# Plain loads of the next batch between the two crossbar parts of a batch, with three smaller moves in the first batch

## The chip, the cores and the metric

The kernel runs on one core of one Trainium2 chip. The metric is the device time of one execution in microseconds; 366.56 us is the median of three runs of the kernel before (366.42 to 367.95).

## The reference

Two stages follow each other. The first is attention with 8 batches, 8 heads, 576 positions and a head size of 64. Heads 0 to 3 ("plain") see the last 32 positions; heads 4 to 7 ("dilated") see every fourth of the last 128. The second is a gated feed-forward block (FFN) over 8 x 576 = 4608 tokens.

```python
B, H, S, D = q.shape                       # 8, 8, 576, 64
scores = (1 / sqrt(D)) * q @ k.transpose(0, 1, 3, 2)
rel = pos[:, None] - pos[None, :]
mask_plain = (rel >= 0) & (rel < 32)                       # heads 0..3
mask_dil = (rel >= 0) & (rel < 128) & (rel % 4 == 0)       # heads 4..7
attn = softmax(where(mask, scores, -1e9)) @ v
x = attn.transpose(0, 2, 1, 3).reshape(B * S, H * D)       # 4608 x 512
g, val = x @ w_gate, x @ w_val                             # 512 -> 1536
out = (gelu(g) * val) @ w_out                              # 1536 -> 512, float32
```

All inputs and the output are float32.

## The kernel before, in words

**Attention** is cut into 32 pairs of heads, n = 0 to 31; batch b is n // 4, so that n = 4b and 4b + 1 are the plain pairs of batch b, and 4b + 2 and 4b + 3 the dilated ones. `emit_s` computes the scores of a pair on TensorE (PE) from transposed q and k and takes their exp on ScalarE (ACT); `emit_pv` computes the numerator (probabilities times v) and the denominator (probabilities times ones); `norm_r` and `norm_x` divide on VectorE (DVE) and write `xT`, the input of the FFN with its 512 channels on the partitions of four tiles, one per pair of a batch. `den` and `num` do the two halves separately for batches 0 and 1.

**The FFN** runs over 9 chunks c of 512 tokens. `ffn1` computes gate and value for one of 12 blocks nb of 128 hidden units into two banks of PSUM (the accumulators, 8 banks), `geglu` forms the product `u_all` on ACT and DVE, and `ffn2` multiplies it with `w_out` for the four groups of 128 tokens; `store` copies a result to one of four `osb` buffers and writes it out from SyncE's queue (SP). `ffn1_two` is the form that takes the first two blocks together, channel tile by channel tile, so that it can begin before all of `xT` is there; it is used for the first blocks of chunks 0 to 2. The scores of later pairs are put between the matmuls of earlier chunks by lists (`in_a`, `in_b`): n = 4 to 7 within chunk 0, 8 to 12 at and after the end of chunk 1's first half, 13 to 19 in chunk 2, 20 to 23 in chunk 3, and so on. PE takes all of it in the order in which it is written.

**Loading a batch b >= 2** has several parts. Float32 rows of q, k for the plain heads come to the tile `st` in 10 transfers, those of v to `sv` in 5, all from SP (`load_batch_plain`: L185 and L173). The dilated rows come to `qd` and `rd` by casting transfers from GpSimd's queue (POOL), and `st` is cast to `qp` by POOL (L190, L191). Then SP issues the crossbar transposes, DMA transfers that transpose fp16 data: two for the dilated heads (`qd`, `rd` to `qTd`: L218, L219) and five for the plain heads (`qp` to `qTp`: L223). At last POOL loads the dilated v (`vd`, `vr`) and casts `sv` (L177, L178). The tiles `st`, `sv`, `qp`, `qd` and `rd` have one buffer each, the transposed tiles two, and those of v three. `last_keys` copies the last 64 keys of the dilated heads to `kTr`; it is done on VectorE (L245) except for batch 0, where it is on POOL, behind the issue of the weights' transfers.

The order of all queues is written by hand (`manual_schedule`); the framework adds the waits. A DMA queue takes its transfers in the order written:

```python
if c in (1, 2, 3):
    load_batch(c + 2)          # plain loads, dilated loads, cast, crossbar, v
if c == 4:
    load_batch(7)
...
    if c == 3 and nb == 5:
        load_batch(6)
```

Batch 2 is loaded in two halves, its plain loads ahead of chunk 0 (`half2`) and the rest after chunk 0's first half. Batch 0 and the q, k of batch 1 are transposed on PE. The first pairs of batch 0 are in this order: den 1, scores 2, den 2, scores 3, num 0 in banks 4 and 5, num 1 in banks 0 and 1, den 3, num 2 in banks 2 and 3, num 3 in banks 4 and 5; `ffn1_two` of chunk 0 uses banks 0, 1, 6 and 7.

Of the kernel before, what the change touches and what calls it, by code (L numbers as in the profile page):

```python
# [38 lines left out]
def kernel(  # L39
# [10 lines left out]
    nc = tc.nc  # L50
# [109 lines left out]
    def new_v(b):  # L160
        vp = vpl.tile([P, 4, HK, D], F16, tag="vp", name=f"vp{b}")
        vd = vpl.tile([P, HK, 4, D], F16, tag="vd", name=f"vd{b}")

        vt = vpl.tile([P, HK, D], F16, tag="vt", name=f"vt{b}")
        vr = vpl.tile([P, HK, 2, D], F16, tag="vr", name=f"vr{b}")
        sv = ldp.tile([P, 5, HK, D], F32, tag="sv", name=f"sv{b}")
        tiles["v", b] = (vp, vd, vt, vr)
        return sv

    def v_plain(b, sv, eng):  # L170
        for kb in range(5):
            k0 = min(kb * P, S - P)
            gated(eng.dma_start(out=sv[:, kb], in_=v[b, 0:HK, k0 : k0 + P, :].rearrange("h p d -> p h d")))  # L173
# [6 lines left out]
    def load_qk_plain(b):  # L180
        st = ldp.tile([P, 5, 2, HK, D], F32, tag="st", name=f"st{b}")
        for t, src in ((0, q), (1, k)):
            for kb in range(5):
                n, sr = rows(src, b, kb)
                gated(nc.sync.dma_start(out=st[0:n, kb, t], in_=sr))  # L185
        return st

    def cast_qk_plain(b, st):
        qp = ldp.tile([P, 5, 2, HK, D], F16, tag="qp", name=f"qp{b}")
        nc.gpsimd.tensor_copy(qp[:, 0:4], st[:, 0:4])  # L190
        nc.gpsimd.tensor_copy(qp[0:64, 4], st[0:64, 4])  # L191
        return qp

    def load_qk_dil(b):
        qd = ldp.tile([P, 2, HK, 4, D], F16, tag="qd", name=f"qd{b}")
        rd = ldp.tile([16, 2, HK, 4, D], F16, tag="rd", name=f"rd{b}")
        for t, src in ((0, q), (1, k)):
            nc.gpsimd.dma_start(out=fl(qd[:, t]), in_=quads(src, b, HK, 0, 4 * P))
        for t, src in ((0, q), (1, k)):
            nc.gpsimd.dma_start(out=fl(rd[:, t]), in_=quads(src, b, HK, 4 * P, S))  # L200
        return qd, rd

    def load_v_dil(b):
        nc.gpsimd.dma_start(out=fl(tiles["v", b][1]), in_=quads(v, b, HK, 0, 4 * P))
        load_v_dil_rest(b)
# [5 lines left out]
                in_=quads(v, b, HK, S - 256, S)[:, :, 2 * m * D : 2 * m * D + 2 * D],  # L211
            )

    def crossbar(b, qp, qd, rd):
        new_qt(b)
        qtp_, qtd_, ktr = tiles["qT", b]
        dst = qtd_.rearrange("p t h m i -> p (t h m) i")
        nc.sync.dma_start_transpose(out=dst[:, :, 0:P], in_=qd.rearrange("p t h r d -> p (t h r d)"))  # L218
        nc.sync.dma_start_transpose(out=dst[:, :, P:NCL], in_=rd.rearrange("p t h r d -> p (t h r d)"))  # L219
        dst = qtp_.rearrange("p t h c -> p (t h) c")  # L220
        for kb in range(5):
            n = min(P, S - kb * P)
            nc.sync.dma_start_transpose(  # L223
                out=dst[:, :, kb * P : kb * P + n], in_=qp[0:n, kb].rearrange("p t h d -> p (t h d)")
            )

    def load_batch_plain(b):
        st = load_qk_plain(b)
        sv = new_v(b)
        v_plain(b, sv, nc.sync)  # L230
        return st, sv

    def load_batch_rest(b, st, sv):
        qd, rd = load_qk_dil(b)
        qp = cast_qk_plain(b, st)
        crossbar(b, qp, qd, rd)
        load_v_dil(b)
        v_cast(b, sv)

    def load_batch(b):  # L240
        load_batch_rest(b, *load_batch_plain(b))

    def last_keys(b, h0, h1, eng=nc.vector):
        _, qtd_, ktr = tiles["qT", b]
        eng.tensor_copy(ktr[:, h0:h1], qtd_[:, 1, h0:h1, :, NCL - 64 : NCL])  # L245


    def is_plain(n):
# [332 lines left out]
    def num(n, b0):  # L581
        emit_pv(n, b0, ("num",))
        norm_x(n, b0)
# [7 lines left out]
        t_dil(0, hp, qd0, 4096 + 1024 * hp, 4608 + 1024 * hp, ("act", "dve"))  # L591
    for hp in range(2):
        t_rest(0, hp, first_r, P * hp)
    last_keys(0, 0, HK, nc.gpsimd)
    den(1, 4, wide=True)
    emit_s(2, 0, pe_mask=True)
    den(2, 4, wide=True)
    emit_s(3, 0, pe_mask=True)
    num(0, 4)
    num(1, 0)  # L600
    den(3, 4, wide=True)
    num(2, 2)
    num(3, 4)


    gate["dma"] = w1
# [15 lines left out]
    load_v_dil(1)  # L622
    v_cast(1, sv1)
    gate["dma"] = wo2
    half2 = load_batch_plain(2)

    mm0 = 0
    in_a = {2: ((4, 12),), **{c: tuple(zip((1, 3, 5, 7), range(NHP * (c + 1), NHP * (c + 2)))) for c in range(3, B - 1)}}
    in_b = {0: range(4, 8), 1: range(8, 13), 2: range(13, 20), **{c: range(NHP * (c + 2), NHP * (c + 3)) for c in range(3, B - 2)}}
    for c in range(NCH):  # L630
        if c in (1, 2, 3):
            load_batch(c + 2)
        if c == 4:
            load_batch(7)
        pv_at = dict(in_a.get(c, ()))
        s_list = list(in_b.get(c, ()))
        pairs = (mm0, mm0 + 2)
        SB = 4 - mm0

        masks = []  # L640
        pend = None
        for nb in range(NNB):
            if nb == 0 and c < 2:
                ffn1_two(c, (0, 6) if c == 0 else (6, 0))
            elif nb == 0 and c == 2:
                ffn1_two(c, pairs)
            elif nb > 1 or c > 2:
                ffn1(c, nb, pairs[(nb + (c < 2 or c == 3)) % 2])
            if pend is not None:
                norm_x(pend, SB)  # L650
                pend = None
            if nb in pv_at:
                pend = pv_at[nb]
                emit_pv(pend, SB, wide=True)
                norm_r(pend, SB, wide=True)
            if c == 0 and nb in (8, 9):
                t_plain(1, q61, nb - 8, 4 + 2 * (nb - 8), ("act", "dve"))
            if c == 0 and nb in (10, 11):
                rr = rd1.rearrange("p t h r d -> p t (h r d)")
                hp = nb - 10  # L660
                t_dil(1, hp, qd1, 4096 + 512 * hp, 5120 + 512 * hp, ("dve", "dve"))
                t_rest(1, hp, (rr[:, 0], rr[:, 1]), 6144 + P * hp)
            if c == 3 and nb == 5:
                load_batch(6)
            if nb == NNB - 1 and c > 0 and s_list:
                masks.append(emit_s(s_list.pop(0), SB))

        def s_next():
            if s_list:
                n = s_list.pop(0)  # L670
                masks.append(emit_s(n, SB, pe_mask=n in (6, 7)))

        def mask_next():
            mask = masks.pop(0) if masks else None
            if mask is not None:
                mask()

        def norm(n, b0):
            norm_r(n, b0)
            norm_x(n, b0)  # L680


        V = mm0 + 1

        def md(n):
            mask_next()
            den(n, 0, wide=True)

        if c == 0:
            load_batch_rest(2, *half2)  # L690
            ffn2(c, 0, 0, {5: [s_next]})
            store(c, 0, 0, "act")
            ffn2(c, 1, 1, {4: [s_next], 8: [lambda: md(4)]})
            store(c, 1, 1, "act")
            s_next()
            ffn2(c, 2, 0, {4: [lambda: md(5)], 6: [s_next], 9: [lambda: md(6)]})
            store(c, 2, 0, "act")
            ffn2(c, 3, 1, {2: [lambda: md(7), lambda: num(4, 4)], 8: [lambda: num(5, 6)]})
            store(c, 3, 1, "act")
            num(6, 2)  # L700
            num(7, 4)
        elif c in (1, 2):

            v0 = 8 if c == 1 else 13

            def pv(n, more=True):
                emit_pv(n, V)
                if more:
                    mask_next()
                norm(n, V)  # L710

            mask_next()
            ffn2(c, 0, V)
            store(c, 0, V, "act")
            s_next()
            ffn2(c, 1, mm0, {6: [lambda: pv(v0)]})
            store(c, 1, mm0, "act")
            s_next()
            ffn2(c, 2, mm0, {4: [lambda: pv(v0 + 1)]})
            store(c, 2, mm0, "act")  # L720
            s_next()
            ffn2(c, 3, mm0, {2: [lambda: pv(v0 + 2)], **({8: [s_next]} if c == 2 else {})})
            store(c, 3, mm0, "act")
            s_next()
            if c == 1:
                pv(v0 + 3, False)
                mm0 = 4 - mm0
            else:
                s_next()
            while masks:  # L730
                mask_next()
        else:
            mask_next()
            ffn2(c, 0, mm0)
            store(c, 0, mm0, "act")
            ffn2(c, 1, mm0 + 1, {5: [s_next]})
            mask_next()
            store(c, 1, mm0 + 1, "act")
            ffn2(c, 2, mm0 + 2, {0: [s_next]})
            mask_next()  # L740
            ffn2(c, 3, mm0 + 3, {0: [s_next]})
            mask_next()
            store(c, 2, mm0 + 2, "act")
            store(c, 3, mm0 + 3, "dve")
# [28 lines left out]
```

## Time and profile before

| what | value |
|---|---|
| median of three runs | 366.56 us |
| profiled execution, own time | 368.56 us |
| its span, first to last instruction | 366.4 us |
| PE busy | 343.0 us (94%) |
| VectorE, ACT, POOL busy | 195.4, 143.5, 76.7 us |
| SP's queue of transfers (q1) | 31.21 MB, 41.2% of 16 engines' span |
| POOL's queue of transfers (q0) | 12.01 MB, 26.9% |
| chunk 0 begins (first `ffn1_two` matmul) | 31.54 us |
| chunk 1 begins | 72.59 us |
| chunk 2 begins | 113.76 us |
| first store's issue | 80.62 us |

The profiled execution is one of its own, with its own time; 2.2 us of it lie outside the span. Times in the profile count from the span's start. "SPq" rows are transfers as SP issues them: their length is the issue, and the landing comes later and is given apart. In brackets after a row stands how long its engine was idle before it, and what ended that. A digit of a busy row is the busy share, in tenths, of one of 40 slices of 9.16 us.

### The profile page before, as it was taken

How to read it: one execution, taken by the hardware profiler on the slowest of the kernel's cores; microseconds unless marked ns; L12 is line 12 of the kernel's file. 1: busy time of each engine (PE TensorE's matmuls, PEld its weight loads, DVE VectorE, ACT ScalarE, POOL GpSimd, SP SyncE). 2: the span in 40 equal slices, each digit the busy share in tenths (PEclk: the TensorE clock that was granted, in tenths of full speed). 3: DMA queues.
4: the chain of work that ended last, by engine and by line, in shares of the span. 5: the costliest groups of instructions: out<-in, count | busy, mean ns of one | idle time of the engine just before them, and what ended most of it. 6: DMA issues, size and time to landing. Idle time of an engine off the chain costs nothing.

```text
span 366.4 us, 5947 instructions
## 1 busy us (share of the span) xinstructions
PE 343.0 (94%) x2340; PEld 162.6 (44%) x2340; DVE 195.4 (53%) x294; ACT 143.5 (39%) x209; POOL 76.7 (21%) x105
## 2 busy tenths in 40 slices
PE   6739999999997999899799999999999999999995
PEld 2515454444443444444344444444444444444442
DVE  1537455843486636789446963696269504303320
ACT  2613346343535254642463256325632313322321
POOL 2680424530630620035062060000000000000000
PEclk9856999999999999999999999999999999999999
DMA  8999999999999991289999996100110020011002
GB/s 211 226 195 225 172 164 179 185 173 247 168 160 226 181 160 59 86 184 160 162 179 150 258 171 134 59 0 3 58 58 0 2 105 10 2 58 57 2 29 86
DMA packets 107291, 45.30 MB, mean 124 GB/s; under 512 B 83040, under 2 KB 102496, under 8 KB 107264
## 3 DMA queue, kind: packets, MB, share of 16 engines
q1 hardware_dynamic: 84272, 31.21, 41.2%
q0 software_dynamic: 21456, 12.01, 26.9%
q10 hardware_dynamic: 1536, 1.70, 2.0%
q8 instruction: 18, 0.29, 0.4%
q14 instruction: 9, 0.07, 0.1%
HBM read 40.13 MB, written 9.44 MB: 135 GB/s over the span
## 4 chain that ended last, share of the span: by engine, by line
PE 67%; DMA 12%; SPq 8%; DVE 5%; POOL 3%; issue 2%; ACT 2%; ACTq 0%; POOLq 0%; DVEq 0%
PE ps L485 35%; PE ps L516 22%; DMA qTp<-qp 4%; SPq L223 4%; PE ps L437 4%; DMA xT<-in_k_dram 3%; SPq L185 3%; PE ps L497 2%; DMA sv<-in_v_dram 2%; DMA out_dram<-osb 2%; PE ps L364 1%; DVE xT L473 1%; DVE u_all L510 1%; PE ps L334 1%; DMA st<-in_k_dram 1%
## 5 line engine op out<-in xcount | busy, mean ns | idle before, releaser
L509 ACT ACTIVATE g<-ps 128x512 f16<-128x512 f32 x108 | 64.0, 597 | 131.9 <-PE ps L485 125.6
L510 DVE SCALAR_TENSOR_TENSOR u_all<-g,ps 128x512 f16<-128x512 f16 x108 | 73.9, 688 | 75.6 <-PE ps L485 68.6
L485 PE MATMUL ps<-xT,wg 128*128 128x512 f16 x408 | 104.9, 379 | 0.2
L485 PE MATMUL ps<-xT,wv 128*128 128x512 f16 x408 | 104.7, 379 | 0.0
L516 PE MATMUL ps<-wo,u_all 128*128 128x512 f16 x432 | 100.1, 380 | 1.7 <-ACT osb L527 1.2
L485 PEld LDWEIGHTS <-wv 128*128 128x128 f16 x408 | 39.9, 98 | 48.1
L516 PEld LDWEIGHTS <-u_all 128*128 128x128 f16 x432 | 39.6, 98 | 46.5 <-issue 1.8
L485 PEld LDWEIGHTS <-wg 128*128 128x128 f16 x408 | 38.2, 98 | 46.1 <-issue 2.5
L527 ACT ACTIVATE osb<-ps 128x512 f32<-128x512 f32 x30 | 17.9, 597 | 43.1 <-PE ps L516 43.1
L455 DVE STREAM_TRANSPOSE dt<-ps 128x576 f32<-128x576 f32 x32 | 24.9, 779 | 12.1 <-PE ps L437 11.5
L190 POOL CAST qp<-st 128x2048 f16<-128x2048 f32 x6 | 11.4, 1903 | 87.7 <-DMA st<-in_k_dram 87.7
L366 ACT ACTIVATE P<-ps 128x1152 f16<-128x1152 f32 x16 | 18.0, 1128 | 19.3 <-PE ps L364 19.3
L459 DVE STREAM_TRANSPOSE rb<-rc 128x576 f32<-128x576 f32 x32 | 24.9, 778 | 1.1
L374 DVE TENSOR_TENSOR P<-P,mask_p 128x1344 f16<-128x1344 f16 x14 | 12.7, 906 | 22.2 <-ACT P L345 22.2
L529 DVE TENSOR_SCALAR osb<-ps 128x512 f32<-128x512 f32 x6 | 4.2, 692 | 30.9 <-PE ps L516 30.9
L344 ACT ACTIVATE P<-ps 128x960 f16<-128x960 f32 x16 | 15.5, 970 | 9.5 <-PE ps L334 9.4
L473 DVE TENSOR_TENSOR xT<-ps,rb 128x576 f16<-128x576 f32 x16 | 17.9, 1125 | 0.2
L374 DVE TENSOR_TENSOR P<-P,mask_d 128x1152 f16<-128x1152 f16 x12 | 10.5, 874 | 12.1 <-ACT P L366 12.1
L437 PE MATMUL ps<-P,ones 128*64 128x288 f16 (+5 forms) x188 | 15.1, 267 | 1.6 <-ACT P L366 1.2
L470 DVE TENSOR_TENSOR xT<-ps,rb 128x576 f16<-128x576 f32 x16 | 11.9, 750 | 1.2 <-PE ps L437 1.1
L334 PE MATMUL ps<-qTp 64*128 64x160 f16 (+2 forms) x160 | 8.0, 221 | 4.1 <-DMA qTp<-qp 4.1
L177 POOL CAST vp<-sv 128x1024 f16<-128x1024 f32 x8 | 8.9, 1107 | 10.9 <-DMA sv<-in_v_dram 10.9
(74 smaller groups left out, 238.0 us busy)
## 6 DMA issues: line engine op xcount, KB each, us to landing
out_dram<-osb SPq DMA_DIRECT2D x36, 256.0 KB, 2.0
sv<-in_v_dram SPq DMA_DIRECT2D x40, 128.0 KB, 3.5
st<-in_q_dram SPq DMA_DIRECT2D x24, 128.0 KB, 5.3
st<-in_k_dram SPq DMA_DIRECT2D x24, 128.0 KB, 3.3
qd<-in_q_dram POOLq DMA_DIRECT2D x7, 256.0 KB, 5.7
qd<-in_k_dram POOLq DMA_DIRECT2D x7, 256.0 KB, 7.3
vd<-in_v_dram POOLq DMA_DIRECT2D x7, 256.0 KB, 6.5
wg<-in_moe_w_gate_dram POOLq DMA_DIRECT2D x3, 512.0 KB, 7.7
```

The source lines that it names most:

```text
L344: nc.scalar.activation(pt[:, :, 0:PB], sb[:, 0, :, 0:PB], AF.Exp, bias=0.0, scale=scale)
L366: nc.scalar.activation(pt, ps[:, b0 : b0 + 4, 0:DW], AF.Exp, bias=0.0, scale=scale)
L374: nc.vector.tensor_tensor(pt, pt, mb, ALU.mult)
L437: nc.tensor.matmul(o, lhs, rhs, start=st, stop=True, skip_group_check=True)
L455: nc.vector.transpose(dst, den)
L459: nc.vector.transpose(rb.rearrange("p (b c) -> p b c", c=32), bass.AP(tensor=rc.tensor, offset=rc.offset, ap=[rc.ap[0], [1, 18], [0, 32]]),)
L473: nc.vector.tensor_tensor(dst.rearrange("p (i m s) -> p i m s", m=2, s=2), num, rb.rearrange("p (s m i) -> p i m s", s=2, m=2), ALU.mult,)
L485: nc.tensor.matmul(ps[:, b0 + gi, :], w[:, kc, ns], xT[kc][:, tok], start=(kc == 0), stop=(kc == NKC - 1))
L509: nc.scalar.activation(g, ps[:, b0, :], AF.Gelu)
L510: nc.vector.scalar_tensor_tensor(u_all[:, nb, :], g, USCALE, ps[:, b0 + 1, :], ALU.mult, ALU.mult)
L516: nc.tensor.matmul(ps[:, bank, :], u_all[:, fc, tb * P : (tb + 1) * P], wo_t[fc // 4][:, fc % 4, :], start=(fc == 0), stop=(fc == NNB - 1),)
L527: nc.scalar.activation(osb, ps[:, bank, :], AF.Copy, bias=0.0, scale=1.0 / USCALE)
```

## The change

`load_batch_rest` becomes the one function for batches 2 to 7. It issues the two dilated transposes of batch b, then the 15 plain loads of batch b + 1 (if there is one), then the five plain transposes of batch b. So batch b + 1 no longer has plain loads at its own place in the chunk loop. POOL's part of a batch keeps its order; its program text stands ahead of the transposes. Three moves concern the first batch: its last keys are copied by VectorE; num 0 comes ahead of den 2, num 1 ahead of den 3 and in banks 4 and 5, num 2 and num 3 in banks 0, 1 and 2, 3; and `ffn1_two` of chunk 0 takes banks 4 to 7. The number of transfers and of matmuls is the same.

```diff
--- before.py
+++ after.py
@@ -211,12 +211,26 @@
                 in_=quads(v, b, HK, S - 256, S)[:, :, 2 * m * D : 2 * m * D + 2 * D],
             )
 
-    def crossbar(b, qp, qd, rd):
+    def load_batch_plain(b):
+        st = load_qk_plain(b)
+        sv = new_v(b)
+        v_plain(b, sv, nc.sync)
+        return st, sv
+
+    def load_batch_rest(b):
+
+        st, sv = tiles["plain", b]
+        qd, rd = load_qk_dil(b)
+        qp = cast_qk_plain(b, st)
+        load_v_dil(b)
+        v_cast(b, sv)
         new_qt(b)
-        qtp_, qtd_, ktr = tiles["qT", b]
+        qtp_, qtd_, _ = tiles["qT", b]
         dst = qtd_.rearrange("p t h m i -> p (t h m) i")
         nc.sync.dma_start_transpose(out=dst[:, :, 0:P], in_=qd.rearrange("p t h r d -> p (t h r d)"))
         nc.sync.dma_start_transpose(out=dst[:, :, P:NCL], in_=rd.rearrange("p t h r d -> p (t h r d)"))
+        if b + 1 < B:
+            tiles["plain", b + 1] = load_batch_plain(b + 1)
         dst = qtp_.rearrange("p t h c -> p (t h) c")
         for kb in range(5):
             n = min(P, S - kb * P)
@@ -224,25 +238,9 @@
                 out=dst[:, :, kb * P : kb * P + n], in_=qp[0:n, kb].rearrange("p t h d -> p (t h d)")
             )
 
-    def load_batch_plain(b):
-        st = load_qk_plain(b)
-        sv = new_v(b)
-        v_plain(b, sv, nc.sync)
-        return st, sv
-
-    def load_batch_rest(b, st, sv):
-        qd, rd = load_qk_dil(b)
-        qp = cast_qk_plain(b, st)
-        crossbar(b, qp, qd, rd)
-        load_v_dil(b)
-        v_cast(b, sv)
-
-    def load_batch(b):
-        load_batch_rest(b, *load_batch_plain(b))
-
-    def last_keys(b, h0, h1, eng=nc.vector):
+    def last_keys(b, h0, h1):
         _, qtd_, ktr = tiles["qT", b]
-        eng.tensor_copy(ktr[:, h0:h1], qtd_[:, 1, h0:h1, :, NCL - 64 : NCL])
+        nc.vector.tensor_copy(ktr[:, h0:h1], qtd_[:, 1, h0:h1, :, NCL - 64 : NCL])
 
 
     def is_plain(n):
@@ -591,16 +589,16 @@
         t_dil(0, hp, qd0, 4096 + 1024 * hp, 4608 + 1024 * hp, ("act", "dve"))
     for hp in range(2):
         t_rest(0, hp, first_r, P * hp)
-    last_keys(0, 0, HK, nc.gpsimd)
+    last_keys(0, 0, HK)
     den(1, 4, wide=True)
     emit_s(2, 0, pe_mask=True)
+    num(0, 4)
     den(2, 4, wide=True)
     emit_s(3, 0, pe_mask=True)
-    num(0, 4)
-    num(1, 0)
+    num(1, 4)
     den(3, 4, wide=True)
-    num(2, 2)
-    num(3, 4)
+    num(2, 0)
+    num(3, 2)
 
 
     gate["dma"] = w1
@@ -622,16 +620,16 @@
     load_v_dil(1)
     v_cast(1, sv1)
     gate["dma"] = wo2
-    half2 = load_batch_plain(2)
+    tiles["plain", 2] = load_batch_plain(2)
 
     mm0 = 0
     in_a = {2: ((4, 12),), **{c: tuple(zip((1, 3, 5, 7), range(NHP * (c + 1), NHP * (c + 2)))) for c in range(3, B - 1)}}
     in_b = {0: range(4, 8), 1: range(8, 13), 2: range(13, 20), **{c: range(NHP * (c + 2), NHP * (c + 3)) for c in range(3, B - 2)}}
     for c in range(NCH):
         if c in (1, 2, 3):
-            load_batch(c + 2)
+            load_batch_rest(c + 2)
         if c == 4:
-            load_batch(7)
+            load_batch_rest(7)
         pv_at = dict(in_a.get(c, ()))
         s_list = list(in_b.get(c, ()))
         pairs = (mm0, mm0 + 2)
@@ -641,7 +639,7 @@
         pend = None
         for nb in range(NNB):
             if nb == 0 and c < 2:
-                ffn1_two(c, (0, 6) if c == 0 else (6, 0))
+                ffn1_two(c, (4, 6) if c == 0 else (6, 0))
             elif nb == 0 and c == 2:
                 ffn1_two(c, pairs)
             elif nb > 1 or c > 2:
@@ -661,7 +659,7 @@
                 t_dil(1, hp, qd1, 4096 + 512 * hp, 5120 + 512 * hp, ("dve", "dve"))
                 t_rest(1, hp, (rr[:, 0], rr[:, 1]), 6144 + P * hp)
             if c == 3 and nb == 5:
-                load_batch(6)
+                load_batch_rest(6)
             if nb == NNB - 1 and c > 0 and s_list:
                 masks.append(emit_s(s_list.pop(0), SB))
 
@@ -687,7 +685,7 @@
             den(n, 0, wide=True)
 
         if c == 0:
-            load_batch_rest(2, *half2)
+            load_batch_rest(2)
             ffn2(c, 0, 0, {5: [s_next]})
             store(c, 0, 0, "act")
             ffn2(c, 1, 1, {4: [s_next], 8: [lambda: md(4)]})
```

## The prediction

> **What bounds the kernel now.** I read the page first, then PE's waits, PE's timeline, SP's timeline and the chain of waits.
>
> ```profile
> PE 343.0 (94%) x2340; PEld 162.6 (44%) x2340; DVE 195.4 (53%) x294; ACT 143.5 (39%) x209; POOL 76.7 (21%) x105
> DMA  8999999999999991289999996100110020011002
> ```
>
> PE is the engine with little idle time (366.4 - 343.0 = 23.4 us). The DMA row is full from slice 1 to 14 (9 to 137 us) and again from 165 to 220: in those stretches a transfer put ahead of another makes the other late.
>
> ```profile
> PE ps L364 <- POOL kTr L245: 4.3, 1, 4.3
> PE ps L334 <- DMA qTp<-qp: 4.1, 3, 1.9
> ...
> 24.06 0.21 PE L364 MATMUL ps<-qTd,kTr 64*128 64x32 f16 x2 [4.34 <-POOL kTr L245]
> ...
> 93.71 0.47 PE L334 MATMUL ps<-qTp 64*128 64x160 f16 x10
> ...
> 112.50 0.20 PE L334 MATMUL ps<-qTp 64*128 64x64 f16 x2 [1.48 <-DMA qTp<-qp]
> ...
> 180.86 0.20 PE L334 MATMUL ps<-qTp 64*128 64x64 f16 x2 [1.93 <-DMA qTp<-qp]
> ```
>
> These are PE's two largest waits and four places of its timeline. The scores of head pair n take batch n // 4. 93.71 is n=8 (batch 2; no wait), 112.50 is n=12 (batch 3; 0.73 + 1.48 us of waiting), 180.86 is n=20 (batch 5). So at the end of chunk 1 PE has **no slack** against the plain crossbar transposes of batch 3, at the end of chunk 3 none against those of batch 5.
>
> ```profile
> 69.19 3.52 SPq L218 DMA_TRANSPOSE qTd<-qd  x1
> 72.83 1.15 SPq L219 DMA_TRANSPOSE qTd<-rd  x1
> 74.08 6.45 SPq L223 DMA_TRANSPOSE qTp<-qp  x5
> 80.62 2.75 SPq L531 DMA_DIRECT2D out_dram<-osb  x4
> 83.42 5.30 SPq L185 DMA_DIRECT2D st<-in_q_dram  x5
> 88.77 3.61 SPq L185 DMA_DIRECT2D st<-in_k_dram  x5
> 92.48 2.76 SPq L173 DMA_DIRECT2D sv<-in_v_dram  x5
> 95.84 2.83 SPq L218 DMA_TRANSPOSE qTd<-qd  x1
> 98.79 1.15 SPq L219 DMA_TRANSPOSE qTd<-rd  x1
> 100.04 6.43 SPq L223 DMA_TRANSPOSE qTp<-qp  x5
> ```
>
> SP's queue from batch 2 to batch 3 has no pause: each row starts where the last ends. Not PE but this queue sets 112.45. The chain of waits says the same:
>
> ```profile
> 80.62 6.31 DMA out_dram<-osb
> 86.94 1.78 SPq L185
> ...
> 105.27 7.18 DMA qTp<-qp
> ```
>
> A store issued at 80.62 lands at 86.93, just after the last transpose before it (79.33 + 7.0 = 86.3, landing from the tile view of qTp). The fifth load of st, eight transfers after that store, issues at that moment: as built, nearly every transfer of SP waits for the landing of the one eight before it.
>
> **The Trainium skill.** "DMA: Bandwidth & Descriptors", Queues, rings and completion order, says that each DMA engine consumes descriptors in ring order and that SP has one row of rings; the store above agrees. Its section Issuing engines are not separate DMA queues says that transfers of all issuers share 16 engines; the trace agrees (the last qTp of batch 2 takes 7.0 us with POOL's qd loads issued at 78.0, the first, ahead of them, 4.4). "TensorE: Matmul & The Clock Gate", Part 1, says that an idle window of about 3.4 us halves the clock and some 3.4 us of work restores it; PE's timeline shows 0.50 from about 16 to 33 us, with matmuls of 512 columns spaced 0.43 us in place of 0.216.
>
> **The change, part by part.**
>
> *Start.* POOL's copy of kTr (661 ns at 23.34, behind four weight issues) becomes one on VectorE: 286 ns, the mean of the seven others there. VectorE is idle for 0.41 us after the qTd copies (17.94 to 18.36), so the copy fits and den(1) is not delayed. Scores n=2 then run at about 19.7, not 24.06: minus 4.34. num(0) and num(1) fill PE's waits for exp (1.23, 0.52); the new banks 4 to 7 of the first FFN step are free in time (norm_x(1) near 25.4, the den(3) read near 26.6). I set FFN start at 27.4 against 31.54: minus 4.1 to 4.9, taken as 4.3. Weights allow it (wv: 16.39 + 8.8 = 25.2). Batch 1's casts end at 43.2 and 44.7 for transposes that would come at 43.7 and 45.9; wo2 lands at 53.1 for a use near 54. So chunk 1 also runs 4.3 early. It lasts only until PE next waits for SP.
>
> *n=8.* SP's new order from 72.83 is: qTd rest of batch 2, 15 plain loads of batch 3, five qTp of batch 2, four stores, two qTd of batch 3, 15 loads of batch 4, five qTp of batch 3. One st tile remains, so the first load waits for the cast of batch 2, done at 70.6: no wait. sv needs the casts that end at 73.9: none. The price of 15 loads: 14 x 128 KB = 1.835 MB at 196 GB/s (mean of 72.6 to 113.76) is **9.4 us**. Checks: 15 loads took 12.4, 11.4, 9.9 and 12.6 us of SP's time at 83.42, 110.79, 153.13 and 173.77; the floor is 15 x 0.51 = 7.7. qTp of batch 2 moves from 86.3 to 95.7. PE comes to n=8 at 93.7 - 4.3 = 89.4 and waits 6.3: the start's gain is gone. Behind it in PE's queue are all of chunk 1's second FFN matmuls, and ACT and VectorE wait for those.
>
> *n=12.* Before, qTp of batch 3 had stores and loads 3 ahead of it; now it has the same **and loads 4**, 15 more transfers: 112.45 + 9.4 = 121.9. The earlier st of batch 3 does not help, since its cast writes the one qp tile, which is free only when qTp of batch 2 has landed (95.7). Cast then 98.2, while stores and qTd of batch 3 still fill the ring, so no further bubble. PE comes to n=12 at 95.7 + 16.1 = 111.8 and waits 10.1 in place of 2.2. After such a wait the clock is at half: about 3.4 us of slow matmuls, **plus 1.7** (estimate by the clock page; from 0, if it holds, to 3.4).
>
> *After n=12.* A batch of SP and DMA work takes 26.7 us before (74.08 to 100.04 to 126.79), so qTp of batch 4 lands near 149; n=16 needs it near 150.5 + 11 = 161. No wait. In chunk 3 the loads of batch 5 have gone into the idle stretch of 137 to 153; loads of batch 6 take their place ahead of qTp of batch 5, but POOL's v loads (0.75 MB) leave this stretch. It lands near 187 for a use near 190: the wait of 1.93 goes, **minus 1.9** (0 to 1.9). The last batch has no loads between its crossbars; four stores after six earlier transfers still precede any reuse of osb. Nothing later waits for DMA. At the end nothing changes.
>
> *Sum.* 9.4 + 1.7 - 1.9 = **+9.2 us**, on the profiled span 366.4. That execution took 368.56 in all (2.2 outside the span), 2.0 above the median 366.56; I add the difference to the median: **375.8**.
>
> **Rivals.**
>
> *Issue-bound, not slower.* If only SP's issue counts and rings keep up: 73.98 + 7.7 + 6.5 + 1.6 + 4.1 + 7.7 + 6.4 = 108.0, and the last qTp, issued at 106.8, lands 3.4 later (the shortest landing of batch 2): 110.2. With the queue's 50 ns pauses that is about 111.5 and the total minus 1.0 minus 1.9: **363.7**. The loads taken before to 95.24 needed 11.8 us where 7.7 would do, and might lose their waits for stores. It decides if 15 loads cost under about 8 us of ring time together with POOL's qd loads. Against it: DMA is full until 137, and qd loads now meet the plain loads.
>
> *Contention twice.* Each block of loads costs 12.6 (as at 173.77, behind transposes, under POOL's loads), and the first block's excess is not caught up: qTp of batch 3 near 126, plus 1.7, and n=20 keeps its wait: **381.9**. For it: the row at 173.77. Against it: part of that time is waiting for transposes that the chain pays anyway.
>
> *The start's edit does nothing.* If n=2 found another wait (exp, weights), PE would come to n=8 later, but still before 95.7 for any loss up to 6.3: total **375.8** all the same. That gain shows only where DMA has slack, which it has not.
>
> **How the numbers follow.** Forecast 0.73 (370 to 381), issue-bound 0.13 (362 to 367), contention twice 0.12, all else 0.02. An unknown of some 4 us either side of +9.2 (loads 7.4 to 12.6, clock 0 to 3.4, n=20 0 to -1.9) gives the forecast's own range. 368 to 382 leaves out the issue-bound case and little above. About 0.5% is what a measurement of this kernel can tell from no change. Faster 0.10, same 0.05 (partly hidden loads), slower 0.85.
>
> **What would show it.** In the changed profile: no wait of PE for kTr and FFN start near 27.4; a PE wait for qTp of 4 to 8 us near 90 and one of 8 to 13 near 112, then a PEclk digit below 9; SP's loads between the two kinds of transpose taking 8 to 13 us; no wait at n=20. Wrong if qTp of batch 3 lands by 113, or if the chain no longer passes through qTp before the second chunk's end.

## The result, and the profile after

The changed kernel is **slower**: 378.93 us (median of four runs, 375.96 to 379.29) against 366.62; the ratio of the means is 1.031, with a 95% interval of 1.0252 to 1.0368. The forecast was 375.8, with a range of 368 to 382. The profiled execution took 378.67 us, 376.9 of it span. A ratio counts only executions within 1.5% of the fastest of the same kernel, which leaves out six of e1's 12 and eleven of e5's 22 below; a median counts them all.

The page of the changed kernel, rows for PE, its clock and DMA:

```profile
PE 348.3 (92%) x2340; PEld 163.8 (43%) x2340; DVE 196.6 (52%) x295; ACT 143.5 (38%) x209; POOL 76.6 (20%) x104
PEclk9959999999697799999999999999999999999999
DMA  8999999999996994549989994100110020011002
```

The same matmuls now take 5.3 us more busy time (348.3 against 343.0): in slices 10 to 13 (94 to 132 us) the clock row has a 6 and two 7s that were not there. In the DMA row slices 15 to 17 have a 4, a 5 and a 4 where they had a 1, a 2 and an 8, and slice 12 (113 to 122 us) has a 6 where it had a 9.

PE's waits and its timeline in the changed kernel (in brackets the idle time before a row):

```profile
PE ps L332 <- DMA qTp<-qp: 13.4, 8, 5.6
...
91.24 0.24 PE L332 MATMUL ps<-qTp 64*128 64x160 f16 x2 [2.49 <-DMA qTp<-qp]
...
94.84 0.24 PE L332 MATMUL ps<-qTp 64*128 64x64 f16 x2 [0.73 <-DMA qTp<-qp]
95.01 5.30 PE L514 MATMUL ps<-wo,u_all 128*128 128x512 f16 x12
...
118.28 0.32 PE L332 MATMUL ps<-qTp 64*128 64x160 f16 x2 [5.59 <-DMA qTp<-qp]
...
121.93 0.24 PE L332 MATMUL ps<-qTp 64*128 64x64 f16 x2 [0.74 <-DMA qTp<-qp]
```

The wait for `kTr` is gone, and waits for `qTp` have grown from 4.1 to 13.4 us. They stand at n=8 (5.2 us in four pieces) and at n=12 (8.2 us in four pieces), as the transposes land one after the other. The 12 matmuls behind n=8 take 5.30 us, where the same row took 2.75 before: the clock is at half. There is no wait at n=20 any more.

The stretch around n=12 in steps of 2 us. After the length of a step stand PE's busy time with its matmuls, the clock that PE was granted, the time of the DMA packets begun in the step as a share of 16 engines' time (packets overlap, so it can pass 1), and GB/s:

```profile
110.00:112.00 2.00, 2.00 (x24) 1.00 1.33 245
112.00:114.00 2.00, 0.68 (x4) 1.00 0.67 141
114.00:116.00 2.00, 0.00 (x0) 1.00 0.97 216
116.00:118.00 2.00, 0.00 (x0) 0.83 0.70 127
118.00:120.00 2.00, 0.63 (x4) 0.50 0.59 117
120.00:122.00 2.00, 0.49 (x6) 0.50 0.30 62
122.00:124.00 2.00, 2.00 (x24) 0.50 1.03 381
```

The clock falls in the fifth microsecond after PE ran out of work at 112.7. And DMA is not full while PE waits: its share lies between 0.30 and 0.97, after 1.33 just before.

SP's queue in the changed kernel:

```profile
73.80 4.00 SPq L185 DMA_DIRECT2D st<-in_q_dram  x5
77.84 3.65 SPq L185 DMA_DIRECT2D st<-in_k_dram  x5
81.59 4.54 SPq L173 DMA_DIRECT2D sv<-in_v_dram  x5
86.18 7.52 SPq L237 DMA_TRANSPOSE qTp<-qp  x5
...
100.92 4.30 SPq L185 DMA_DIRECT2D st<-in_q_dram  x5
105.26 5.08 SPq L185 DMA_DIRECT2D st<-in_k_dram  x5
110.44 3.85 SPq L173 DMA_DIRECT2D sv<-in_v_dram  x5
114.34 6.45 SPq L237 DMA_TRANSPOSE qTp<-qp  x5
```

Two blocks of 15 loads stand ahead of the plain transposes of batch 3 where one stood before. They hold SP for 12.4 us (73.80 to 86.18) and 13.4 us (100.92 to 114.34). The chain of waits passes from these transposes to PE:

```profile
107.56 2.79 SPq L185
...
119.54 2.34 DMA qTp<-qp
121.93 0.24 PE ps L332 x2
```

The last `qTp` of batch 3 is issued at 119.54 and lands at 119.54 + 2.34 = 121.88. One load, at 107.56, holds the queue for 2.79 us.

### The profile page after: what moved, and what is told of

Read it like the earlier page. It is cut to its first block, busy times and chain, and to the rows that moved or that the text cites. A ratio compares the mean times of both kernels' runs of the same rounds, so it can differ in the third digit from the quotient of the medians.

```text
span 376.9 us, 5936 instructions
## 1 busy us (share of the span) xinstructions
PE 348.3 (92%) x2340; PEld 163.8 (43%) x2340; DVE 196.6 (52%) x295; ACT 143.5 (38%) x209; POOL 76.6 (20%) x104
## 4 chain that ended last, share of the span: by engine, by line
PE 59%; DMA 14%; SPq 13%; DVE 7%; POOL 4%; issue 2%; ACT 1%; ACTq 0%; POOLq 0%; DVEq 0%
PE ps L483 34%; PE ps L514 18%; SPq L185 6%; SPq L173 4%; DMA xT<-in_k_dram 3%; PE ps L435 3%; SPq L237 3%; DMA sv<-in_v_dram 3%; DMA st<-in_k_dram 3%; DMA wv<-in_moe_w_val_dram 3%; PE ps L495 2%; DMA wo<-in_moe_w_out_dram 1%; DVE u_all L508 1%; DVE xT L471 1%; DMA qTp<-qp 1%
## 5 line engine op out<-in xcount | busy, mean ns | idle before, releaser
L514 PE MATMUL ps<-wo,u_all 128*128 128x512 f16 x432 | 102.7, 387 | 1.2 <-ACT osb L525 1.2
L453 DVE STREAM_TRANSPOSE dt<-ps 128x576 f32<-128x576 f32 x32 | 24.9, 779 | 13.4 <-PE ps L435 12.8
L372 DVE TENSOR_TENSOR P<-P,mask_p 128x1344 f16<-128x1344 f16 x14 | 13.7, 979 | 28.1 <-ACT P L343 28.1
L332 PE MATMUL ps<-qTp 64*128 64x160 f16 (+2 forms) x160 | 9.0, 227 | 13.4 <-DMA qTp<-qp 13.4
L332 PEld LDWEIGHTS <-qTp 64*128 64x128 f16 x160 | 5.5, 95 | 21.6 <-DMA qTp<-qp 10.7
```

What stands on the lines that cost most here:

```text
L372: nc.vector.tensor_tensor(pt, pt, mb, ALU.mult)
L453: nc.vector.transpose(dst, den)
L514: nc.tensor.matmul(ps[:, bank, :], u_all[:, fc, tb * P : (tb + 1) * P], wo_t[fc // 4][:, fc % 4, :], start=(fc == 0), stop=(fc == NNB - 1),)
```

## The experiments

The theory under test, **order**: what stands ahead of the plain transposes of batch 3 in SP's queue sets the start of chunk 2, and with it the end. Its rivals: the time comes from DMA being full wherever the loads stand; the moves of the first batch carry part of it; PE's clock, or a collision of engines, does.

One table first. Chunk 2 begins with the first matmul of its `ffn1_two`; "rest" is the span minus that moment. All are from one profiled execution each.

| kernel | chunk 2 begins | span | rest |
|---|---|---|---|
| before | 113.76 | 366.4 | 252.6 |
| changed | 123.25 | 376.9 | 253.7 |
| e1, e9: loads after the transposes | 111.58, 109.83 | 364.1, 362.1 | 252.5, 252.3 |
| e2: start moves only | 112.64 | 365.5 | 252.9 |
| e3: loads moved only | 124.31 | 378.1 | 253.8 |
| e4: only v between | 113.93 | 365.3 | 251.4 |
| e5, e10: and chunk 0's stores late | 108.68, 111.70 | 360.9, 365.4 | 252.2, 253.7 |
| e6: changed, with added matmuls | 122.92 | 374.8 | 251.9 |
| e7: changed, with a cast held | 121.76 | 374.9 | 253.1 |
| e8: start moves, with added matmuls | 113.34 | 365.4 | 252.1 |
| e11: e5, and v after the transposes | 109.10 | 361.2 | 252.1 |

The rest lies within 2.4 us in all of them, the start of chunk 2 within 15.6 us. Most of what decides is done by the start of chunk 2. Two executions of one kernel differ there by 1.75 us (e1, e9) and 3.02 (e5, e10), so smaller differences between single profiles show nothing.

**e1, the loads after the plain transposes.** In `load_batch_rest`:

```diff
-        if b + 1 < B:
-            tiles["plain", b + 1] = load_batch_plain(b + 1)
         dst = qtp_.rearrange("p t h c -> p (t h) c")
         for kb in range(5):
...
+        if b + 1 < B:
+            tiles["plain", b + 1] = load_batch_plain(b + 1)
```

> The changed kernel with one edit: the 15 plain loads of batch b+1 stand after the five plain transposes of batch b, not ahead of them. Order theory (the loads ahead of the plain transposes are what makes qTp late): qTp of batch 2 lands near 86 and of batch 3 near 112, PE waits 0 at n=8 and some 8 us at n=12 (it arrives 5.7 us early and the transfers do not), no wait at n=20; total about 364 to 365. Start rival (the moves of the first batch are worth their 5.7 us whenever the loads don't interfere): 360 to 361. Contention rival (any earlier load of a batch hurts, wherever it stands, since DMA is full): 372 or more.

Measured: a median of 368.73 us (363.05 to 372.32) against 366.86 for the kernel before in the same series, and a ratio of 0.9983 (0.9945 to 1.002). The median lies 0.5% above the kernel before and the ratio 0.2% below it: no difference from it can be told. The loss of 3% is gone. PE's timeline of e1:

```profile
107.47 0.30 PE L332 MATMUL ps<-qTp 64*128 64x160 f16 x4 [0.30 <-DMA qTp<-qp]
110.33 0.20 PE L332 MATMUL ps<-qTp 64*128 64x64 f16 x2 [2.56 <-DMA qTp<-qp]
```

Moving the 15 loads over five transposes gives back 11.7 us at the start of chunk 2 in the profile: no wait at n=8, none at n=20, the last `qTp` of batch 3 landed at 110.3. That refutes the contention rival in its strong form, since the loads are still earlier than before. POOL's part of a batch stands where the changed kernel has it, so its new place in the program is not the cause either. PE waited 2.9 us at n=12 and not 8, for two reasons: the transposes landed 2.2 us earlier than in the kernel before (112.45), and PE arrived near 107 and not 104. I had carried the whole 5.7 us of the start to n=12, but of 4.6 us at chunk 0 (26.91 against 31.54) 3.7 were left at n=8 (90.05 against 93.71) and 2.8 at n=12 (106.86 against 109.68). The total of 364 to 365 was missed by the profiled execution (366.07) and by the median: long executions exist, and their cause in this kernel is open.

**e9, the same kernel, a second profile.**

> The kernel with the loads after the plain transposes once more, for a second profile, since its times lie between 363 and 372 us. Order theory: in a long execution the wait at n=12 (or n=8) is longer by what the time is longer, with a half clock after it. Rival (VectorE and POOL collide): the wait at n=12 is the same and mask products of about 2 us hold PE elsewhere.

It fell on a short execution (364.05 us; waits for `qTp` of 0.6 us), so it doesn't tell what the long ones of e1 do.

**e2, only the moves of the first batch**, on the kernel before:

```diff
-    last_keys(0, 0, HK, nc.gpsimd)
+    last_keys(0, 0, HK)
...
-    num(0, 4)
-    num(1, 0)
+    num(1, 4)
...
-                ffn1_two(c, (0, 6) if c == 0 else (6, 0))
+                ffn1_two(c, (4, 6) if c == 0 else (6, 0))
```

> The kernel before with only the moves of the first batch (last keys on VectorE, order and banks of the numerators and of the first FFN step). Order theory: chunk 0 begins at 25.8 in place of 31.5, but PE meets the same qTp of batch 3 at 112.5: wait of about 8 us at n=12, total 366 to 367, no gain that can be measured. Rival (the gain of the start reaches the end): 361.

Measured: 368.37 us, a ratio of 1.0046 (1.0019 to 1.0073). Chunk 0 begins at 26.84 in place of 31.54, chunk 2 at 112.64 in place of 113.76, and its first scores (n=13) at 135.63 in place of 135.75. The gain of the start does not reach the end; the kernel is even slower by 0.5%. In PE's timeline of e2, n=12 waits 4.3 us in place of 2.2, not the 8 that were expected:

```profile
108.02 0.25 PE L334 MATMUL ps<-qTp 64*128 64x160 f16 x2 [1.50 <-DMA qTp<-qp]
110.60 0.30 PE L334 MATMUL ps<-qTp 64*128 64x160 f16 x4 [2.34 <-DMA qTp<-qp]
111.38 0.20 PE L334 MATMUL ps<-qTp 64*128 64x64 f16 x2 [0.48 <-DMA qTp<-qp]
```

**e3, only the new place of the loads**: the diff of the change without the three moves of the first batch.

> The kernel before with only the new place of the plain loads; the first batch as before. Order theory: qTp of batch 3 lands near 122 as in the changed kernel, PE arrives later and waits less, total 376 to 379, the same as the changed kernel. Rival (start moves carry part of the time): differs from the changed kernel by 4 to 6 us, to 382 to 384.

Measured: 379.18 us, a ratio of 1.0333 (1.0295 to 1.0371), the same as the changed kernel's 1.031. The last `qTp` of batch 3 lands at 122.9. The loads' place carries the whole loss, the start moves none of it that these runs can tell.

**e4, a dose: only v's five loads between.**

```diff
         if b + 1 < B:
-            tiles["plain", b + 1] = load_batch_plain(b + 1)
+            sv1_ = new_v(b + 1)
+            v_plain(b + 1, sv1_, nc.sync)
         dst = qtp_.rearrange("p t h c -> p (t h) c")
...
+        if b + 1 < B:
+            tiles["plain", b + 1] = load_qk_plain(b + 1), sv1_
```

> The changed kernel, but of the 15 plain loads only the 5 of v stand between the two kinds of transposes; the 10 of q and k come after the plain transposes. Order theory with the bytes as price: 640 KB at 196 GB/s = 3.3 us later than with none, qTp of batch 3 near 115 to 116, total near 368 to 369, a third of the way from the order with none between to the changed kernel. Rival (a threshold: what counts is the wait of the loads for st, cast or the eight transfers in flight, not the amount): no shift at all (364 to 365) or the whole one (376 and more).

Measured: 368.70 us, a ratio of 1.0055 (1.0035 to 1.0076). Chunk 2 begins at 113.93, 2.4 us after e1's 111.58 and 4.1 after e9's; the changed kernel is 11.7 and 13.4 after them. In these profiles 5 of 15 transfers (640 of 1792 KB) cost 20 to 31% of the shift, neither none nor all of it: that speaks for the amount and against a threshold. The times do not confirm it. The medians of e4 and e1 can't be told apart, so the rival's "no shift" is refuted by the profiles alone, and the last `qTp` landed at 112.6, short of the expected 115 to 116.

**e5, chunk 0's four stores behind the plain transposes of batch 3**, on e1, with seven `osb` buffers in place of four:

```diff
-        nc.sync.dma_start(out=out[t0 : t0 + P, :], in_=osb)
+        if c == 0:
+            late.setdefault(3, []).append(lambda: nc.sync.dma_start(out=out[t0 : t0 + P, :], in_=osb))
+        else:
+            nc.sync.dma_start(out=out[t0 : t0 + P, :], in_=osb)
```

> Loads after the plain transposes, as in the first experiment, and chunk 0's four stores (1 MB) moved behind the plain transposes of batch 3, with seven osb buffers in place of four. Order theory (every transfer ahead of qTp of batch 3 costs its ring time): 1 MB less ahead is 3 to 5 us less, qTp of batch 3 lands near 106 to 108, PE waits 1 to 3 us at n=12, total 360 to 363. Rival (PE-bound once the loads are out of the way): the same 364 to 367 as without the moved stores.

Measured: a median of 365.96 us (360.61 to 367.95) against 366.94, and a ratio of 0.9925 (0.99 to 0.9951). By the median that is 0.3% below the kernel before, by the ratio 0.75%; the median lies where the rival put it. In the profile, a short execution, the last `qTp` of batch 3 lands at 106.5, as the theory had it, and PE waits for none at n=12. The added buffers alone were not tried.

**e10, the same kernel, a second profile.**

> The kernel with chunk 0's stores late once more, for a second profile, since its times lie between 360 and 368 us. Order theory: a long execution has a wait for qTp of batch 3 at n=12 that the first profile of it (360.9 us of span) did not have. Rival: no such wait, and the time lies in chunk 0 or in mask products.

This one is long, 367.35 us. PE's timeline of e10:

```profile
108.17 0.30 PE L335 MATMUL ps<-qTp 64*128 64x160 f16 x4 [2.34 <-DMA qTp<-qp]
109.73 0.20 PE L335 MATMUL ps<-qTp 64*128 64x64 f16 x2 [1.26 <-DMA qTp<-qp]
111.70 0.59 PE L498 MATMUL ps<-xT,wg 128*128 128x512 f16 x1 [1.11 <-ACT P L345]
```

The wait at n=12 is back, and the first matmul of chunk 2 takes 0.59 us, at half clock. The last `qTp` landed 3.2 us later than in e5's profile, chunk 2 begins 3.0 us later, its first scores 5.6 (136.26 against 130.67), and 4.5 of it are left in the span. The same code thus waits for these transfers in one execution and not in another: in this pair, that is the spread. Why the transfers came later is open.

**e11, also v behind the transposes**, on e5, for batches 3 to 7:

```diff
-        load_v_dil(b)
-        v_cast(b, sv)
...
+        if b > 2:
+            sv = new_v(b)
+            v_plain(b, sv, nc.sync)
+            load_v_dil(b)
+            v_cast(b, sv)
```

> The kernel with chunk 0's stores late, and the v loads (plain, dilated) and casts of batches 3 to 7 behind their own batch's plain transposes: another 640 KB from SP and 512 + 256 KB from POOL less ahead of qTp of batch 3. Order theory: qTp of batch 3 lands 3 to 6 us earlier, no wait at n=12 in any execution, 360 to 362. Rival (PE is the bound by then, or v now comes late for the first numerators of batch 3): 363 or more.

Measured: 363.17 us (360.75 to 365.49), a ratio of 0.9887 (0.9836 to 0.9939). It is the fastest version found, 1.1% below the kernel before; against e5 the intervals overlap. The total lies on the rival's side of 363. In the profile the last `qTp` of batch 3 lands at 101.8, 4.7 us before e5's, as the theory had it, and PE does not wait for it; but chunk 2 begins no earlier (109.10 against 108.68). What PE waits for there is VectorE (0.87 us) and ACT (0.94): the queue has stopped being the limit.

**e6, the clock.** 40 matmuls of ones ahead of the scores of n=12, in the changed kernel:

```diff
+            if c == 1:
+                warm(40, 4)
             s_next()
```

> The changed kernel with 40 matmuls of ones (8.6 us of PE work into a bank that n=12 overwrites) put ahead of the scores of n=12, where PE waits anyway. Clock theory (the wait drops PE's clock and 2 us of chunk 2 are lost to it): no digit below 9 in the clock row near 122 to 128, the first FFN step of chunk 2 takes 3.5 us and not 5.3, total 2 us below the changed kernel, 376 to 377. Rival (the loss after the wait comes from elsewhere, or the added work delays n=12): no change or more, 378 to 381.

Measured: 376.88 us, a ratio of 1.0284 (1.0233 to 1.0335). The intervals of e6 and of the changed kernel overlap, so the total settles nothing. The profile does. PE's timeline of e6:

```profile
111.49 8.80 PE L533 MATMUL ps<-ones 128*128 128x512 f16 x40
120.22 0.57 PE L332 MATMUL ps<-qTp 64*128 64x160 f16 x8
121.67 0.20 PE L332 MATMUL ps<-qTp 64*128 64x64 f16 x2 [0.87 <-DMA qTp<-qp]
122.92 0.38 PE L495 MATMUL ps<-xT,wg 128*128 128x512 f16 x1 [0.40 <-ACT P L342]
```

The last transpose lands when it did (121.6), and chunk 2 begins within 0.3 us of when it did, but its first matmul takes 0.38 and not 0.61 us. The first FFN step lasts 3.85 us (122.92 to 126.77) against 5.78 in the changed kernel (123.25 to 129.03): the half clock cost 1.9 us there. The rest of the span is shorter by 1.8.

**e8, the same on e2**, with 22 matmuls.

> The kernel with only the moves of the first batch, and 22 matmuls of ones (4.7 us) ahead of the scores of n=12. Clock theory (the start's gain is turned into a longer wait at n=12, which drops the clock and makes that kernel 1 to 2 us slower than before): total 366 to 367, 1.5 us below the same kernel without them. Rival (qTp of batch 3 itself comes later in that kernel): no change, near 368.

Measured: 367.25 us, a ratio of 1.0001 (0.998 to 1.0022) against e2's 1.0046 (1.0019 to 1.0073). By the medians, work that computes nothing makes e2 faster by 1.1 us; the two intervals just touch. The profiles show where: in e2 chunk 2 begins 1.12 us before that of the kernel before and its first scores only 0.12 us, so the half clock took 1.0; in e8 the two leads are 0.42 and 0.43. That explains why nothing is left of the start's gain. That e2 is 0.5% slower is not explained by it, and stays open: e2's profiled span is no longer than that of the kernel before (365.5 and 366.4), nor than e8's (365.4).

**e7, a collision.** The cast of batch 5 waits for chunk 2's last store:

```diff
-        nc.gpsimd.tensor_copy(qp[:, 0:4], st[:, 0:4])
+        cast = nc.gpsimd.tensor_copy(qp[:, 0:4], st[:, 0:4])
+        if b == 5:
+            tc.add_manual_dep(cast.ins, tiles["st_c2"].ins.name, SYNC, reason="order of casts")
```

> The changed kernel with one added dependency: POOL's cast of batch 5's q and k waits for the last store of chunk 2 (near 165 us), and so does all of POOL behind it. Collision theory (VectorE's two mask products of 2.23 us near 150 and the PE wait of 0.97 us at 157 come from POOL's casts at 149 to 156): those products take 0.76 to 0.86 again, the PE wait is gone, total 1 us below the changed kernel. Rival (they come from elsewhere): products stay long, total the same; or the later cast holds up the loads of batch 6 and qTp of batch 5, and the total rises by 1 us or more.

The timelines of VectorE and POOL in the changed kernel:

```profile
149.73 2.23 DVE L372 TENSOR_TENSOR P<-P,mask_p 128x1344 f16<-128x1344 f16 x1 [1.67 <-ACT P L343]
152.05 2.23 DVE L372 TENSOR_TENSOR P<-P,mask_d 128x1152 f16<-128x1152 f16 x1
...
149.35 1.89 POOL L190 CAST qp<-st 128x2048 f16<-128x2048 f32 x1 [15.03 <-DMA qTp<-qp]
151.19 1.24 POOL L191 CAST qp<-st 64x512 f16<-64x512 f32 x1
```

and VectorE in e7:

```profile
148.07 0.86 DVE L374 TENSOR_TENSOR P<-P,mask_p 128x1344 f16<-128x1344 f16 x1 [1.67 <-ACT P L345]
150.39 0.76 DVE L374 TENSOR_TENSOR P<-P,mask_d 128x1152 f16<-128x1152 f16 x1 [1.46 <-ACT P L366]
```

Measured: 377.05 us, a ratio of 1.0302 (1.0254 to 1.0351): no difference in the total that these runs can tell. Inside, the two products are short again and PE's wait of 0.97 us at 157 is gone. From n=13 to n=17 PE takes 14.64 us (145.54 to 160.18), as in the kernel before (14.63), and not 15.68: the collision is real and cost 1.05 us. In exchange 0.49 us of waiting at n=20 are back, and a later product, at 165, takes 2.08 us beside the moved cast. The rest falls by 0.5 us (253.65 to 253.14), which is too little for single profiles to show.

## Why the prediction was right, point by point

*What bounds the kernel.* Right: no slack at n=12, and SP's queue sets that moment, as e1 and e3 show. One reading was too wide. The forecast said that nearly every transfer of SP waits for the landing of the one eight before it. That held for two loads (86.35 and 86.94) of the kernel before. In the changed kernel the load at 107.56 held SP for 2.79 us though the transfer eight before it had landed at 106.78. What makes single loads take over 2 us to issue is open.

*Start.* Forecast 27.4 for the first FFN matmul, measured 25.83; the copy of `kTr` on VectorE took no place on the path. That the gain would be lost is shown by e2 and e3. In e2 a part of it (1.0 us) goes to the clock, which the forecast did not have. The third rival said 375.8 for a start that gains nothing, and e3, which has no such gain, has the changed kernel's time.

*n=8.* Forecast: `qTp` of batch 2 at 95.7, PE there at 89.4. Measured 94.8 (92.45 + 2.35) and 88.75; the waits come to 5.2 us, with pieces of the scores between them (forecast 6.3).

*n=12.* Forecast: the last `qTp` of batch 3 at 121.9. Measured 121.88. The number held better than its working. The price of 9.4 us was bytes over the mean rate, for a ring that stays full. What the trace shows is two terms: the last transpose is issued 14.27 us later (119.54 against 105.27), and it lands 2.34 us after its issue and not 7.18, since DMA is no longer full by then. The difference is 9.43. That it meets 9.4 so closely is luck in part: with the same order in SP's queue the landing is at 120.4 in e7 and 122.9 in e3. PE came at 112.7 and not 111.8. It left n=8 0.9 us earlier than forecast, but the half clock behind n=8 cost it 2.55 us (5.30 against 2.75), a term that the forecast put at nothing. It did not count in the end, since PE then waits at n=12 anyway.

*Rivals.* Issue-bound: refuted by its number, since a block of loads held SP for 12.4 and 13.4 us and not 7.7. But its picture has a part of the truth: behind the second block of loads each transpose lands 2.3 to 3.1 us after SP begins to issue it, so SP's queue sets its time. Contention twice: the blocks did hold SP about as long as it said (12.6), but the last `qTp` landed at 121.88 and not near 126, and the wait at n=20 is gone. It is gone by little: the last `qTp` of batch 5 landed at 189.9 for a use at 191.06 (forecast 187 and 190).

*Sum.* PE's rows for n=13 and n=17, before and after:

```profile
135.75 0.47 PE L334 MATMUL ps<-qTp 64*128 64x160 f16 x10
150.38 0.47 PE L334 MATMUL ps<-qTp 64*128 64x160 f16 x10
...
147.20 0.47 PE L332 MATMUL ps<-qTp 64*128 64x160 f16 x10
162.88 0.47 PE L332 MATMUL ps<-qTp 64*128 64x160 f16 x10
```

Chunk 2 began 9.49 us late (123.25 against 113.76; forecast 9.4). By its first scores (n=13) it was 11.45, so the clock took 1.96. The forecast had 1.7, an estimate from the window of about 3.4 us that the Trainium skill gives ("TensorE: Matmul & The Clock Gate", Part 1); e6 shows the cost directly. At n=17 it was 12.50: **1.05 us that no step of the forecast had**. Behind n=20 it was 10.46 (195.23 against 184.77), so the wait there gave 2.04 (forecast 1.9). In all 10.5 in the spans, against 9.2.

The missing microsecond is the collision of e7. The forecast looked for a wait of PE for batch 4's late transposes (landed at 148.97, forecast 149) and rightly found none. But the cast of batch 5 waits for them, since there is one `qp` tile; it moved from 162.09 to 149.35, into the softmax work of chunk 2, where it met VectorE. I had followed PE and the queues, and not POOL's casts, to their new time.

*The rest of the difference.* 378.93 - 375.8 = 3.1 us: 1.3 come from the sum, the other 1.8 from its base. The profiled execution before took 368.56 us, 1.9 above the median, and that of the changed kernel 378.67, which is its median but for 0.3. I added the spans' difference to the median; the executions of one kernel differ by about as much. So the total is right within its range, with every large term of the sum near its size; a closer agreement than some 2 us would have been luck.

## What to carry to other kernels

Before moving transfers earlier in an in-order queue, list what falls behind them and ask which of those PE will want first: here 1.8 MB of loads for a later batch went ahead of the transposes for the next scores. A gain ahead of a full queue becomes a longer wait behind it, and a long wait of PE cost 1.0 to 2.6 us more here through the clock (e2, and the matmuls behind n=8). Where PE waits for a queue, take stores and later loads out from ahead of what it waits for (e5, e11), until PE no longer waits: beyond that, e11 gains nothing at chunk 2. And follow every engine that waits for a moved transfer to its new time, not only PE.

## What the runs showed of the hardware that was not expected

A mask product of VectorE (two fp16 inputs in SBUF, 0.76 to 0.86 us) takes up to 2.2 us when it starts during a cast on POOL; the cast of 64 x 512 then takes 1.24 in place of 0.61. The product that starts at 149.73, just after the cast of 149.35, ends at 151.96, 0.72 us after that cast does (151.24): it looks as if it waited for the whole cast and then ran at about its own length. The Trainium skill says so ("SBUF — State Buffer", Terms: the shared port pair of the two engines is held exclusively for an instruction). For this product the runs agree in size, but only timing was seen here, not the port.

The second product, at 152.05, does not fit so simply. The cast that it met ended at 152.43, yet it ran until 154.28. POOL's next rows in the changed kernel are the issues of v's transfers:

```profile
152.38 0.77 POOL L204 DMA_DIRECT2D vd<-in_v_dram  x1
153.14 1.24 POOL L209 DMA_DIRECT2D vr<-in_v_dram  x2
```

They end at 154.38, just after the product. Whether they held it is not shown: e7 moved the casts and these issues together. Such products run long in the kernel before too (1.45 us at 186.65 and 1.89 at 188.54); the change moved the collision to a place where PE waits for it.

PE's clock did not come back while PE did little: in the changed kernel it fell to 0.50 near 93 us, during the waits at n=8 that began at 88.75, stayed there through the pieces of the scores, and returned only near 100 us, five microseconds after full work had begun (95.01). A long wait for a transfer is not needed for the fall: in e11 the first matmul of chunk 2 takes 0.59 us, after waits of at most 0.94 us; PE was busy for 1.3 of the 3 us from 106 to 109. How much idle time it takes, these runs don't tell.
